# Nyström attention and a sticky mixture of experts: another order and another split of batch 0's steps

## The chip, the cores and the metric

One core of one Trainium2 chip runs the kernel. The metric is device time in microseconds of one execution; lower is better. Inputs lie in HBM in float32, and the output is written there in float32.

## The reference, cut

Attention with 32 landmarks per head, for 8 batches, 8 heads, 576 positions and 64 channels; A, Bm and C are softmaxes against landmark means, and Z is an iterated pseudo-inverse of Bm. A mixture of 8 experts follows, in which each token keeps its predecessor's expert unless its gate says otherwise.

```
q_lm, k_lm = means of q and k over 32 segments of 18
A  = softmax(scale * q    @ k_lm.T)      # 576 x 32 per head
Bm = softmax(scale * q_lm @ k_lm.T)      # 32 x 32
C  = softmax(scale * q_lm @ k.T)         # 32 x 576
Z  = Bm.T / (norm1(Bm) * norminf(Bm))
for _ in range(6): Z = 2 * Z - Z @ Bm @ Z
x = A @ Z @ C @ v                        # heads side by side: 576 x 512 per batch
logits, local = x @ w_gate, sigmoid(x @ w_local)
e[s] = argmax(logits[s]) if s == 0 or local[s] < 0.5 else e[s - 1]
out[s] = softmax(logits[s])[e[s]] * (relu(x[s] @ w1[e[s]]) @ w2[e[s]])
```

## The kernel before

All work is written out in one program under a manual order: each engine runs its instructions in the order in which the code issues them, and waits on semaphores for what it needs. For each batch the kernel finds the expert that most of its tokens have, runs that expert's two products for the whole batch (`expert`, with `mm1` for the hidden layer), and later runs the tokens of other experts in extra slots. It never forms x in full: W = Z C v and w1 are first multiplied into G (`w_w1`, and `first_w1` for the first 128 hidden units), so the hidden layer is A times G, in three products of high and low halves (`ath`, `atl`, `gh`, `gl`).

Batch 0's attention is written by hand in `startup`, and it has no other batch's work to hide behind. Its order is: loads of q, k and v of batch 0 and then of batch 1 on SP's queue; filler products on TensorE over zeros (L190, L192); landmark sums on VectorE (L261) and scores of C, Bm and A; then the Newton iteration (`newton` on TensorE, `newton_add` on VectorE, L1062) with the softmax of A between its steps (`sa_max`, `sa_exp`, `sa_sum`, `sa_norm`, `sa_back`). A lies in the tile `sa` in two groups of heads of 128 x 576; `sa_max` takes the maxima on VectorE (L1069) and subtracts them on GpSimd (L1070), `sa_exp` runs on ScalarE, `sa_sum` on VectorE (L1077), `sa_norm` inverts the sums on VectorE (L176, L177) and multiplies on GpSimd (L1081), `sa_back` transposes into `full` on VectorE (L1084). C times v (`c_v_rows`) goes to PSUM as `pv`, and u is `pv` over its sums, on ScalarE (L1127). From u come W, the gate's weights `wgc` (L760), the gate's logits (`gates`, L825), and `vote`, which writes the expert of the batch to `regs` (L875).

Around these steps stand pieces of batch 1's landmarks: `lk0`, `lq2` and `lk2` have halves on GpSimd (L310) and sums on VectorE (L313), `lq0` sums in pieces on VectorE (L294). `keep_busy` issues wide products over ones on TensorE (L930). The tile `firsts` (`w1f`, 2 MB) holds the first 128 hidden units of all eight experts, loaded before the expert is known.

Behind `regs`, SP reads the expert and issues the transfers of w1 (`load_w1`, L1232) and w2 (`load_w2`, L1274). `second_block`, at the simulated time 0.02, makes batch 1's scores of C (`c_products`, L621) and the second 128 units of G (`w_w1`, L1247, casts on ScalarE L1266, low halves `gl` on VectorE L1269); `c_max` takes maxima over those scores on VectorE (L631). `at_time` sets at which step of the expert's loop further pieces are issued; `fresh` (L847 `pe`, L849 `eq`) is one of them. GpSimd makes the low halves of w2 (`wl`, L1284).

## Time and profile before

| | us |
|---|---|
| median of 3 runs (451.6 to 452.22) | 451.7 |
| the profiled execution | 451.21 |
| its span, first to last instruction | 449.4 |
| TensorE busy in the span | 435.1 (97%) |
| VectorE | 284.5 (63%) |
| ScalarE | 216.0 (48%) |
| GpSimd | 192.0 (43%) |

The span is what the trace covers; the other 1.8 us lie around it. A matmul's end is modelled, so TensorE's busy share says little on its own; what counts is where it stands still and what it waits for.

### The profile page before, as it was taken

Reading aid. Unit: us, or ns where it says so; the run is one execution under the profiler, and the core shown is the slowest. Engines: PE = TensorE matmul, PEld = TensorE weight load, DVE = VectorE, ACT = ScalarE, POOL = GpSimd, SP = SyncE. Lnnn points to the kernel's source line nnn. Section 1 sums busy time; section 2 is a strip of 40 time slices with the busy share of each in tenths; the row PEclk is TensorE's granted clock in tenths of the full one; section 3 lists DMA queues with packets and bytes.
Section 4 is the critical chain, followed back from the end, with each engine's and each line's share of the span. In section 5 each row is a group of like instructions: output and inputs, shape, how many; then the busy total and the mean of one; then the engine's idle time right before and its main releaser. Section 6 shows DMA issues by size and latency. Waiting matters only on the chain.

```text
span 449.4 us, 12512 instructions
## 1 busy us (share of the span) xinstructions
PE 435.1 (97%) x4898; PEld 337.1 (75%) x4898; DVE 284.5 (63%) x869; ACT 216.0 (48%) x577; POOL 192.0 (43%) x235
## 2 busy tenths in 40 slices
PE   8888999999999999999999999999999999999996
PEld 3455777777786788878887788788887778776885
DVE  7878786666858576665766574656555786954111
ACT  2546525467354751566253752465145414445611
POOL 5456663165815664263632650174116601055520
PEclk9999999999999999999999999999999999999999
DMA  8959952779569697649957615831164315692211
GB/s 303 378 198 350 367 190 98 268 287 261 210 160 382 202 388 159 245 164 341 290 138 260 237 54 125 318 110 48 55 233 158 113 44 173 252 313 95 97 31 50
DMA packets 62365, 91.53 MB, mean 204 GB/s; under 512 B 26731, under 2 KB 28267, under 8 KB 61152
## 3 DMA queue, kind: packets, MB, share of 16 engines
q1 hardware_dynamic: 60960, 86.23, 57.0%
q0 software_dynamic: 1344, 4.48, 2.7%
q8 instruction: 39, 0.64, 0.6%
q14 instruction: 22, 0.18, 0.1%
HBM read 75.27 MB, written 15.47 MB: 202 GB/s over the span
## 4 chain that ended last, share of the span: by engine, by line
PE 77%; DVE 13%; ACT 5%; issue 2%; DMA 1%; POOL 1%; SPq 0%; DVEq 0%; ACTq 0%; POOLq 0%
PE py L1337 33%; PE ph L1295 19%; PE pg L1346 5%; PE ph L1247 2%; PE one L416 2%; PE one L463 1%; DVE h L1307 1%; PE one L562 1%; PE py L1573 1%; DMA k_t<-kT 1%; PE one L517 1%; DVE gl L1269 1%; PE one L825 1%; POOL t L265 1%; DVE sk L261 1%
## 5 line engine op out<-in xcount | busy, mean ns | idle before, releaser
L1337 PE MATMUL py<-wh,h 128*128 128x512 f32 x504 | 161.6, 403 | 0.1
L1284 POOL TENSOR_TENSOR wl<-raw,wh 128x512 fp32r<-128x512 f32 x64 | 82.2, 1293 | 70.8 <-ACT wh L1282 69.7
L1302 ACT ACTIVATE h<-ph 128x256 fp32r<-128x256 f32 (+1 forms) x128 | 52.4, 413 | 111.2 <-PE ph L1295 94.2
L1337 PEld LDWEIGHTS py<-wh,h 128*128 128x128 f32 x504 | 86.4, 189 | 25.2 <-issue 13.2
L1307 DVE SCALAR_TENSOR_TENSOR h<-ph,h 128x256 fp32r<-128x256 f32 x128 | 53.0, 416 | 61.0 <-ACT h L1302 58.2
L1337 PE MATMUL py<-wl,h 128*128 128x512 f32 x252 | 80.5, 400 | 0.0
L1295 PE MATMUL ph<-ath,gh 128*128 128x320 f32 (+1 forms) x256 | 77.5, 303 | 1.5 <-ACT gh L1266 0.8
L1295 PE MATMUL ph<-ath,gl 128*128 128x320 f32 (+1 forms) x256 | 75.8, 296 | 0.0
L1295 PE MATMUL ph<-atl,gh 128*128 128x320 f32 (+1 forms) x256 | 75.6, 295 | 0.0
L1295 PEld LDWEIGHTS ph<-ath,gh 128*128 128x128 f32 x256 | 48.4, 189 | 9.1 <-ACT h L1302 2.2
L1337 PEld LDWEIGHTS py<-wl,h 128*128 128x128 f32 x252 | 45.9, 188 | 11.6 <-issue 1.3
L1295 PEld LDWEIGHTS ph<-atl,gh 128*128 128x128 f32 x256 | 48.3, 189 | 3.9
L1295 PEld LDWEIGHTS ph<-ath,gl 128*128 128x128 f32 x256 | 48.3, 189 | 0.2 <-DVE gl L1269 0.2
L1282 ACT CAST wh<-raw 128x512 fp32r<-128x512 f32 x69 | 43.2, 627 | 2.2 <-DMA raw<-w 1.4
L1406 POOL TENSOR_TENSOR ys<-ys,yl 64x512 f32<-64x512 f32 x8 | 10.3, 1281 | 58.5 <-ACT yl L1404 58.5
L265 POOL TENSOR_TENSOR t<-q_t 128x288 f32<-128x288 f32 x20 | 14.5, 747 | 23.5 <-DVE sk L267 23.5
L423 DVE TENSOR_TENSOR et<-et,one 128x64 f32<-128x64 f32 x36 | 7.9, 220 | 24.7 <-ACT et L422 16.4
L794 POOL TENSOR_TENSOR sa<-sa,rsa 128x1152 f32<-128x1152 f32 x7 | 14.9, 2133 | 19.9 <-DVE s L693 13.2
L265 POOL TENSOR_TENSOR t<-k_t 128x288 f32<-128x288 f32 x22 | 17.0, 795 | 11.9 <-DVE sq L267 10.8
L1346 PE MATMUL pg<-wl,h 128*128 128x512 f32 x56 | 21.9, 391 | 0.0
L1346 PE MATMUL pg<-wh,h 128*128 128x512 f32 x56 | 21.8, 390 | 0.0
L1395 ACT ACTIVATE ys<-py,token 128x512 f32<-128x512 f32 x30 | 19.0, 685 | 5.0 <-PE py L1337 4.7
(435 smaller groups left out, 729.3 us busy)
## 6 DMA issues: line engine op xcount, KB each, us to landing
raw<-w SPq DMA_DIRECT2D x75, 256.0 KB
raw<-w SPq DMA_DIRECT2D x16, 1024.0 KB
k_t<-kT SPq DMA_DIRECT2D x9, 1152.0 KB
q_t<-qT SPq DMA_DIRECT2D x9, 1152.0 KB
out<-ys SPq DMA_DIRECT2D x31, 256.0 KB
v_t<-v SPq DMA_DIRECT2D x20, 256.0 KB
ad<-sa POOLq DMA_DIRECT2D x7, 576.0 KB, 3.1
v_t<-v SPq DMA_DIRECT2D x3, 1024.0 KB
```

The source lines that it names most:

```text
L265: nc.gpsimd.tensor_add(t9[:, i], src[:, a + i, :, 0:9], src[:, a + i, :, 9:18])
L416: return {1: lambda: each_place(lambda g, r: nc.tensor.matmul(pn[r, g, :], et[r, g, 0:32], et[r, g, n0:64], start=True, stop=True))}, part ...
L794: nc.gpsimd.tensor_tensor(out=sa, in0=sa, in1=rs.unsqueeze(2).broadcast_to([P, 2 * NJ, M]), op=ALU.mult)
L1282: by(out=wh, in_=raw)
L1284: rest.tensor_tensor(out=wl, in0=raw, in1=wh.bitcast(F32), op=ALU.subtract)
L1295: mm = nc.tensor.matmul(hp, w[:, g, c], x[:, g, s0:s0 + n], start=(i == 0), stop=(i == 5))
L1302: nc.scalar.activation(out=h[:, 0:e], in_=hp[:, 0:e], func=AF.Relu)
L1307: nc.vector.scalar_tensor_tensor(out=h[:, 384:384 + m], in0=hp[:, 0:m], scalar=0.0, in1=h[:, 0:m].bitcast(F32), op0=ALU.max, op1=ALU.subtract)
L1337: nc.tensor.matmul(yps[k], h[:, part + i * P:part + i * P + P], w, start=(f == 0 and part == 0 and w is wh), stop=(f == NC2 - 1 and part = ...
L1346: nc.tensor.matmul(yps[4], hs[ff][1], w, start=(ff == 0 and w is w2[ff][0]), stop=(ff == NC2 - 1 and w is w2[ff][1]))
L1395: nc.scalar.mul(out=ys, in_=yp, mul=st["pw"][:, k:k + 1])
L1406: nc.gpsimd.tensor_tensor(out=ys[0:64], in0=ys[0:64], in1=yl[0:64], op=ALU.add)
```

## The change

In words, in the order of the program. The fillers at the start become 12 wide and 35 narrow ones. The 2 MB preload into `firsts` is issued later in SP's queue, behind a one-element memset of that tile on GpSimd that stands after `lk0`'s two halves. Group 1 of A is subtracted, exponentiated, summed, scaled and transposed in two parts, of 9 and 9 of its 18 segments; the inverse of its sums stays one. The sums of C are reduced and inverted two Newton steps sooner. Newton's fourth addition and fifth step come ahead of A's first sum. u is made by one instruction on VectorE in place of two on ScalarE. `lq2`'s halves on GpSimd move behind A's products, and `lk0`'s sums on VectorE move between the transposes. Two fillers in place of three behind C times v; five wide fillers in place of three wide and 22 narrow ones behind the vote. w1's first half comes in two transfers in place of three, the second in one in place of two. `lq0`'s piece ahead of the gate moves behind the expert, where a single piece and a double one stand in place of two single ones. Batch 1's scores of C are issued in two halves, the second behind the second weight product, and the scores of the last 96 columns behind the product for blocks 2 and 3.

```diff
-    for _ in range(11):
+    for _ in range(12):
         nc.tensor.matmul(pz, zeros[:, 0:P], zeros, start=True, stop=True)
-    for _ in range(18):
+    for _ in range(35):
         nc.tensor.matmul(pz[:, 0:16], zeros[:, 0:P], zeros[:, 0:16], start=True, stop=True)
...
-    def c_products(st, k0, n):
+    def c_products(st, k0, n, places=range(4)):
...
-        for c in range(4):
+        for c in places:
...
         firsts = pre.tile([P, E, 512], F32, name="w1f")
-        nc.sync.dma_start(out=firsts, in_=w12[:, 0, :, 0:512].rearrange("e p x -> p e x"))
...
+        whole, first, second = slice(0, NJ), slice(0, 9), slice(9, NJ)
+
         def sa_max(g):
             nc.vector.reduce_max(out=mxa[:, g], in_=sa[:, g], axis=AX.X)
...
+        def sa_scaled(x, g, j, op):
+            nc.gpsimd.tensor_tensor(out=sa[:, g, j], in0=sa[:, g, j],
+                                    in1=x[:, g, j].unsqueeze(2).broadcast_to([P, j.stop - j.start, M]), op=op)
+
+        def sa_exp(g, j=whole):
+            nc.scalar.activation(out=sa[:, g, j], in_=sa[:, g, j], func=AF.Exp, scale=scale)
+
+        def sa_sum(g, j=whole):
+            nc.vector.reduce_sum(out=rsa[:, g, j], in_=sa[:, g, j], axis=AX.X)
+
+        def sa_back(g, j=whole):
+            nc.vector.transpose(out=full[:, g, M * j.start:M * j.stop], in_=sa[:, g, j].rearrange("p j l -> p (j l)"))
...
         sa_max(0)
+        sa_scaled(mxa, 0, whole, ALU.subtract)
         lk0_half(0)
         lk0_half(1)
+        nc.gpsimd.memset(firsts[0:1, 0, 0:1], 0.0)
+        nc.sync.dma_start(out=firsts, in_=w12[:, 0, :, 0:512].rearrange("e p x -> p e x"))
...
         c_turn(4, 1)
+        nc.vector.reduce_sum(out=sums[:, 2:4], in_=sc, axis=AX.X)
+        nc.vector.reciprocal(out=sums[:, 2:4], in_=sums[:, 2:4])
...
         sa_max(1)
+        sa_scaled(mxa, 1, first, ALU.subtract)
+        sa_scaled(mxa, 1, second, ALU.subtract)
+        sa_exp(0)
         c_v_rows(st, pv, 0, range(3, 5))
         c_v_rows(st, pv, 1, range(0, 2))
-        sa_exp(0)
-        sa_sum(0)
         newton_add(4)
         newton(5)
-        nc.vector.reduce_sum(out=sums[:, 2:4], in_=sc, axis=AX.X)
-        nc.vector.reciprocal(out=sums[:, 2:4], in_=sums[:, 2:4])
+        sa_sum(0)
+        sa_exp(1, first)
         c_v_rows(st, pv, 1, range(2, 5))
         idle = ph.tile([P, 512], F32, name="ph")
-        keep_busy(3, idle)
+        keep_busy(2, idle)
+        newton_add(5)
+        inverse(rsa[:, 0], 1e-9)
+        sa_scaled(rsa, 0, whole, ALU.mult)
+        u = st["u"] = sm.tile([P, 2, D], F32, name="u")
+        nc.vector.tensor_tensor(out=u, in0=pv, in1=sums[:, 2:4].unsqueeze(2).broadcast_to([P, 2, D]), op=ALU.mult)
+        sa_exp(1, second)
+        sa_sum(1, first)
+        sa_sum(1, second)
+        inverse(rsa[:, 1], 1e-9)
+        sa_scaled(rsa, 1, first, ALU.mult)
+        sa_scaled(rsa, 1, second, ALU.mult)
         lq2_half(0)
-        sa_norm(0)
-        newton_add(5)
-        sa_exp(1)
-        u = st["u"] = sm.tile([P, 2, D], F32, name="u")
-        for g in range(2):
-            nc.scalar.mul(out=u[:, g], in_=pv[:, g], mul=sums[:, 2 + g:3 + g])
-        sa_sum(1)
-        sa_norm(1)
         lq2_half(1)
         sa_back(0)
-        lk0(0)
...
-        lq0(1)
+        sa_back(1, first)
+        lk0(0)
         newton_gate(0, st)
         keep_busy(2, idle)
-        sa_back(1)
+        sa_back(1, second)
+        lk0(1)
         a_high(1)
...
-        lk0(1)
...
         vote(st, lq0)
-        keep_busy(3)
-        pz = one.tile([P, 512])
-        for _ in range(22):
-            nc.tensor.matmul(pz[:, 0:16], ones, ones[:, 0:16], start=True, stop=True)
+        keep_busy(5)
...
-        st["w1", 0] = load_w1(e, 0, ((nc.sync, 1, 1, 0, P), (nc.sync, 2, 1, 0, P), (nc.sync, 3, 1, 0, P)))
+        st["w1", 0] = load_w1(e, 0, ((nc.sync, 1, 1, 0, P), (nc.sync, 2, 2, 0, P)))
...
-        st["w1", 1] = load_w1(e, 1, ((nc.sync, 0, 2, 0, P), (nc.sync, 2, 2, 0, P)))
+        st["w1", 1] = load_w1(e, 1)
...
         lq0(1)
-        lq0(1)
+        lq0(2)
...
-            c_products(nx, 0, 512)
+            c_products(nx, 0, 512, (0, 1))
             lk2(0)
             lk2(1)
             g1 = w_w1(st, 0, 1, 1, ((py, "py"), (py, "py")))
             next(g1)
-            c_products(nx, 512, 96)
+            c_products(nx, 0, 512, (2, 3))
             c_max(nx, 1, (0,))
             at_once(g1)
...
         at_time(1.005, lambda: at_once(w_w1(st, 0, 2, 2, ((py, "py"), (py, "py")))))
+        at_time(1.007, c_products, nx, 512, 96)
```

VectorE, before, from the maximum over A's group 1 to the transpose of group 0 (`yl` holds Newton's matrices, `mxa` and `rsa` the maxima and sums of A):

```order
L1069 TENSOR_REDUCE mxa<-sa 128x18
L1077 TENSOR_REDUCE rsa<-sa 128x18
L1062 TENSOR_TENSOR yl<-ph,yl 128x2x64
L1116 TENSOR_REDUCE sums<-sc_239 128x2
L1117 RECIPROCAL sums<-sums 128x2
L176 TENSOR_SCALAR rsa<-rsa 128x18
L177 RECIPROCAL rsa<-rsa 128x18
L1062 TENSOR_TENSOR yl<-ph,yl 128x2x32
L1077 TENSOR_REDUCE rsa<-sa 128x18
L176 TENSOR_SCALAR rsa<-rsa 128x18
L177 RECIPROCAL rsa<-rsa 128x18
L1084 STREAM_TRANSPOSE at<-sa 128x576
```

The same stretch of VectorE in the changed kernel:

```order
L1070 TENSOR_REDUCE mxa<-sa 128x18
L1061 TENSOR_TENSOR yl<-ph,yl 128x2x64
L1080 TENSOR_REDUCE rsa<-sa 128x18
L1061 TENSOR_TENSOR yl<-ph,yl 128x2x32
L176 TENSOR_SCALAR rsa<-rsa 128x18
L177 RECIPROCAL rsa<-rsa 128x18
L1130 TENSOR_TENSOR u<-pg,sums 128x128
L1080 TENSOR_REDUCE rsa<-sa 128x9 x2
L176 TENSOR_SCALAR rsa<-rsa 128x18
L177 RECIPROCAL rsa<-rsa 128x18
L1083 STREAM_TRANSPOSE at<-sa 128x576
L1083 STREAM_TRANSPOSE at<-sa 128x288
```

Newton's addition now stands between the maximum and the sum, the sums of C have left, u has come in behind the first inverse, and group 1's sum and transpose are in parts.

GpSimd, before, from the first subtraction of A to the low half of A (`h` are batch 1's landmark halves):

```order
L1070 TENSOR_TENSOR sa<-sa,mxa 128x576
L310 TENSOR_TENSOR h<-k_t_229 128x288 x2
L1070 TENSOR_TENSOR sa<-sa,mxa 128x576
L310 TENSOR_TENSOR h<-q_t_228 128x288
L1081 TENSOR_TENSOR sa<-sa,rsa 128x576 x2
L310 TENSOR_TENSOR h<-q_t_228 128x288
L1148 TENSOR_TENSOR atl<-at,ath 128x576
```

The same stretch of GpSimd in the changed kernel:

```order
L1073 TENSOR_TENSOR sa<-sa,mxa 128x576
L310 TENSOR_TENSOR h<-k_t_247 128x288 x2
L1096 MEMSET w1f 1x1
L1073 TENSOR_TENSOR sa<-sa,mxa 128x288 x2
L1073 TENSOR_TENSOR sa<-sa,rsa 128x576
L1073 TENSOR_TENSOR sa<-sa,rsa 128x288 x2
L310 TENSOR_TENSOR h<-q_t_246 128x288 x2
L1155 TENSOR_TENSOR atl<-at,ath 128x576
```

The memset has come in behind the first landmark halves, the other two halves have moved behind all of A's products, and group 1 is in parts.

TensorE, before, behind the first hidden product of batch 0 (`one` and `pg` receive batch 1's scores, `py` the product with w1):

```order
L1295 MATMUL ph<-atl,gh 128x320
L1295 MATMUL ph<-ath,gl 128x320
L621 MATMUL one<-k_t_229,ql 32x512 x8
L1247 MATMUL py<-raw_620,wt 32x128 x8
L621 MATMUL one<-k_t_229,ql 32x96
L621 MATMUL pg<-k_t_229,ql 32x96
```

The same stretch of TensorE in the changed kernel:

```order
L1301 MATMUL ph<-ath,gl 128x320
L621 MATMUL one<-k_t_247,ql 32x512 x4
L1253 MATMUL py<-raw_620,wt 32x128 x8
L621 MATMUL one<-k_t_247,ql 32x512 x4
L1301 MATMUL ph<-ath,gh 128x320
L1301 MATMUL ph<-atl,gh 128x320
L1301 MATMUL ph<-ath,gl 128x320
```

Half of the wide scores now stand behind the weight product, and the narrow ones have left this place. Each float32 product of this list runs as two in the trace.

## Rows read from the trace of the kernel before

**Rows 1.** Windows: length, busy us of PE PEld DVE ACT POOL, clock, DMA, GB/s

```profile
18.00:24.00 6.00, 5.24 (x154) 2.92 (x154) 5.35 (x16) 2.83 (x8) 5.51 (x7) 1.00 0.97 353
...
36.00:42.00 6.00, 4.97 (x36) 3.17 (x36) 4.80 (x20) 4.55 (x21) 3.97 (x5) 1.00 1.02 371
42.00:48.00 6.00, 6.00 (x76) 3.94 (x78) 5.20 (x19) 3.53 (x11) 3.98 (x5) 1.00 1.03 406
```

**Rows 2.** Chain of waits: start us, length us, engine, tile, line

```profile
7.33 0.37 DVE nm L977
```

**Rows 3.** Timeline of TensorE at the start: start us, length us, instruction, count

```profile
1.23 4.88 PE L190 MATMUL one<-sa 128*128 128x512 bf16 x11 [1.23 <-DVE sa L180]
...
5.90 0.65 PE L192 MATMUL one<-sa 128*128 128x16 bf16 x18
...
6.49 0.69 PE L965 MATMUL one<-k_t,ql 64*32 64x288 f32 x8
```

**Rows 4.** Timeline, 19 to 26 us, all engines

```profile
19.06 0.74 DVE L1069 TENSOR_REDUCE mxa<-sa 128x18 f32<-128x576 f32 x1
...
19.71 0.74 DVE L1077 TENSOR_REDUCE rsa<-sa 128x18 f32<-128x576 f32 x1
19.88 1.16 POOL L1070 TENSOR_TENSOR sa<-sa,mxa 128x576 f32<-128x576 f32 x1
20.37 0.28 DVE L1062 TENSOR_TENSOR yl<-ph,yl 128x128 f32<-128x128 f32 x1
...
20.84 0.23 DVE L176 TENSOR_SCALAR rsa<-rsa 128x18 f32<-128x18 f32 x1
...
20.99 0.74 POOL L310 TENSOR_TENSOR h<-q_t 128x288 f32<-128x288 f32 x1
...
21.66 0.50 ACT L1127 ACTIVATE u<-pg,sums 128x64 f32<-128x64 f32 x2
21.70 1.16 POOL L1081 TENSOR_TENSOR sa<-sa,rsa 128x576 f32<-128x576 f32 x1
...
22.20 0.42 PE L1134 MATMUL ph<-u,yl 32*32 32x64 f32 x16
...
22.57 0.31 DVE L176 TENSOR_SCALAR rsa<-rsa 128x18 f32<-128x18 f32 x1
...
24.74 0.77 DVE L1084 STREAM_TRANSPOSE at<-sa 128x576 f32<-128x576 f32 x1
...
25.96 0.52 PE L825 MATMUL pg<-at,wgc 128*32 128x128 f32 x10 [0.46 <-issue]
```

**Rows 5.** Single lines' instructions: ns min/median/max, first and last start us

```profile
L176 DVE TENSOR_SCALAR rsa<-rsa x9: 182/184/311, 20.8 to 354.2; 128x36 f32<-128x36 f32 x7, 128x18 f32<-128x18 f32 x2
...
L849 DVE SCALAR_TENSOR_TENSOR eq<-pe,keys x8: 199/201/1344, 37.6 to 367.3; 128x40 f32<-128x40 f32 x8
...
L621 PE MATMUL one<-k_t,ql x24: 242/589/613, 31.5 to 32.8; 64*32 64x512 f32 x16, 64*32 64x96 f32 x8
```

**Rows 6.** Timeline, from the expert to 40 us, all engines

```profile
28.19 0.80 DVE L294 TENSOR_REDUCE sq<-q_t 128x16 f32<-128x288 f32 x2
...
29.00 1.43 SPq L1232 DMA_DIRECT2D raw<-w  x3
...
32.39 0.45 PE L1247 MATMUL py<-raw,wt 64*32 64x128 f32 x16
...
32.64 0.69 DVE L631 TENSOR_REDUCE nm8c<-one 128x1 f32<-128x512 f32 x1 [0.86 <-PE one L621]
...
33.25 0.48 DVE L1269 TENSOR_TENSOR gl<-py,gh 128x128 fp32r<-128x128 f32 x2
...
37.58 1.29 POOL L1284 TENSOR_TENSOR wl<-raw,wh 128x512 fp32r<-128x512 f32 x1
37.59 1.34 DVE L849 SCALAR_TENSOR_TENSOR eq<-pe,keys 128x40 f32<-128x40 f32 x1
...
39.94 0.59 PE L1247 MATMUL ph<-raw,wt 64*32 64x512 f32 x1 [0.97 <-DVE atl L1310]
```

More of the change, by code (lines that the diff above doesn't have):

```diff
@@ L1066, in startup @@
         full = st["full"] = at.tile([P, 2, S], F32, name="at")
+        whole, first, second = slice(0, NJ), slice(0, 9), slice(9, NJ)
         def sa_max(g):
             nc.vector.reduce_max(out=mxa[:, g], in_=sa[:, g], axis=AX.X)
-            nc.gpsimd.tensor_tensor(out=sa[:, g], in0=sa[:, g], in1=mxa[:, g].unsqueeze(2).broadcast_to([P, NJ, M]),
-                                    op=ALU.subtract)
-        def sa_exp(g):
-            nc.scalar.activation(out=sa[:, g], in_=sa[:, g], func=AF.Exp, scale=scale)
-        def sa_sum(g):
-            nc.vector.reduce_sum(out=rsa[:, g], in_=sa[:, g], axis=AX.X)
-        def sa_norm(g):
-            inverse(rsa[:, g], 1e-9)
-            nc.gpsimd.tensor_tensor(out=sa[:, g], in0=sa[:, g], in1=rsa[:, g].unsqueeze(2).broadcast_to([P, NJ, M]), op=ALU.mult)
-        def sa_back(g):
-            nc.vector.transpose(out=full[:, g], in_=sa[:, g].rearrange("p j l -> p (j l)"))
+        def sa_scaled(x, g, j, op):
[7 more added lines that the diff above has]
+            nc.vector.transpose(out=full[:, g, M * j.start:M * j.stop], in_=sa[:, g, j].rearrange("p j l -> p (j l)"))
         lq0 = landmark_parts(nx, "q", 0)
```

## The prediction

> **What bounds the kernel now.** I read the windows table first, then the chain of waits and the timeline of the first 45 us, then the instructions of three lines on their own. From 42 us on a window of 6 us holds 6.00 us of TensorE work; the one before holds 4.97, the startup's like it [rows 1]. Past 42 us TensorE waits for nothing that this diff touches, so what the diff does before that point moves the end by as much, with its sign. The profiled execution took 451.21 us for a span of 449.4; the median of the runs is 451.7, half a microsecond above it. I make the sum as shifts against the profiled execution and put the same shifts on the median, because that is what will be compared.
>
> The startup is one serial chain over VectorE, TensorE, ScalarE and GpSimd up to the batch's expert (`regs`), then a second one from the expert to about 40 us. I take the parts in that order.
>
> **Filler at the start.** The fillers stand ahead of the first scores on TensorE: 11 wide ones from 1.23 to 5.90, 0.42 us each, then 18 narrow ones in 0.59, and at 6.49 the first scores follow directly [rows 3]. The maximum over those scores stands on VectorE ahead of the sums of the second half of q and k, and the chain of waits runs through it at 7.33 [rows 2]. So VectorE takes over each delay of these scores. The change adds one wide filler and 17 narrow ones. The narrow ones cost 17 x 0.59/18 = 0.56 at most; the wide one 0.42 at 1.2 GHz (512 columns in 0.42 us, as the eleven before it) or half of that at 2.4 GHz. Ends 0.65 and 1.0; I take 0.8, the middle. A cost of nothing would need data that arrive later than in this execution. Cost **+0.8**.
>
> **Newton, A's sums and u, up to the expert.** Before, A's sum stands ahead of Newton's fourth addition: maximum at 19.06, sum at 19.71 (each 0.74), addition at 20.37 [rows 4]. Now the addition follows the maximum, at 19.72, which is 0.65 sooner; the last product starts 0.05 behind its end, at 20.06, with the sum beside it (19.92 to 20.66), and the last addition comes at 20.6. Then the inverse (0.2 and 0.3) and u on VectorE, 128x128 from PSUM like the addition at 20.37, so 0.28: u ends at 21.45 where ScalarE's two ended at 22.16 (21.66 + 0.50), and the product with u, at 22.20 before, can start at 21.5: 0.7 sooner. That is not yet the gain, because the gate products also need all of A, whose transpose was the later of the two (24.74 + 0.77 = 25.51) [rows 4]. For A I count GpSimd again. A half of 288 elements I price at 0.74, as the 128x288 row at 20.99, against 1.16 for 576: the split adds 0.32 per step. The tiny memset for the preload takes 0.1. So: halves of the subtraction 19.97 to 21.45, group 0's product to 22.65, group 1's inverse ready at 23.0, its halves to 23.8 and 24.55. VectorE transposes group 0 (0.77) from 22.9, then the first half (0.4), one landmark sum (0.4, half of the 0.80 for two at 28.19 [rows 6]), the gate's copy (0.2), and the second half (0.4): A is complete at 25.05. Gain **-0.45** on the expert.
>
> Bounds. After A's end TensorE stood 0.45 us longer (25.51 to 25.96, a row with "issue" [rows 4]); if that stall goes too, the gain is 0.9. The other end is the inverse. Its first instruction, a median of 0.18, took 0.31 at 22.57 and ended at 22.88, just when GpSimd's operation of 21.70 + 1.16 = 22.86 did [rows 4, 5]. With two halves back to back it can be kept off until 21.4; then u gives 0.2 instead of 0.7 and A ends at 25.35: a gain of 0.15.
>
> **After the expert.** The landmark sums behind it on VectorE grow from two pieces (0.80) to one of the same size and a double one, 0.4 + 0.74, so ScalarE's scale and its first cast of G come 0.35 later. That is hidden: only 8 of 16 score products now stand ahead of the second weight product on TensorE (at 32.39, [rows 6]), which frees 0.45, and that product waits for its transfer anyway. Five wide fillers in place of three and 22 narrow ones end some 0.2 sooner; the same casts hide that.
>
> But the other 8 score products now come behind the weight product. VectorE's maximum over them stood at 32.64, with `gl` behind it at 33.25 [rows 6]; in the new order both keep their places, and the maximum cannot start until products that begin at 32.64 and take 0.59 [rows 5] have ended: 33.3, and `gl` at 33.9, 0.65 later. The hidden layer's third product waits for `gl`, the weight product for blocks 2 and 3 stands behind it, and the next `gl` behind that. The 8 small products (512 to 575) that moved away lie in a later TensorE wait and give nothing. The 0.65 then meets the wait at 39.94, where TensorE stands for 0.97 until VectorE is through [rows 6]. There `eq` took 1.34 us from 37.59, next to GpSimd's `wl` from 37.58 to 38.87; its median over the batches is 0.20 [rows 5, 6]. If VectorE comes 0.65 later it finds the same `wl`, stands at `pe` instead of `eq` until 38.87, and is through some 0.35 later than before, not 0.65. Ends: nothing, and the full 0.65. Cost **+0.35**.
>
> The Trainium skill has a rule for this pair, on its page "SBUF — State Buffer", section "Who interferes with whom": VectorE and GpSimd share one pair of SBUF ports, a VectorE instruction with two SBUF inputs, or one in a two-port mode, contends with GpSimd, and whoever comes second is shut out for the other's whole instruction. The rows at 22.57 and 37.59 agree with it: both ended as GpSimd's did. Without it 1.34 us would be read as the price of `eq`, and the cost here would be 0.65 instead of 0.35.
>
> **Transfers.** Held back behind GpSimd's memset (after the two landmark halves, so at 20 + 0.8) the preload's 2.1 MB begin at about 22 and at the 353 GB/s of that stretch [rows 1] take 5.9 us: there at 28. TensorE needs it about when SP issues the first weights, at 29.00 before [rows 6] and 29.35 now. The stores of A and W, 0.7 MB, follow to 29.9, as the first weights' bytes begin. Cost nothing, at most 0.5 where these overlap. Fewer, larger transfers of w1 save issue time on SP, but the engines are full there (share 1.02 from 36 to 42 us [rows 1]), and the product for blocks 2 and 3 needed both anyway: nothing.
>
> **Sum.** 0.8 - 0.45 + 0.35 = +0.7: 451.9 in a profiled execution, **452.4** against the median of 451.7. That is +0.15%, and about 0.2%, 0.9 us, is what a measurement of this kernel can tell from no change.
>
> **Rivals.**
> (a) Slower: GpSimd's halves keep VectorE's inverse off until 21.4, as worked out above. It decides if the second half starts before the inverse asks, about 20.7; both are due within 0.1 us. Then u and A give 0.1 instead of 0.45: 0.8 - 0.1 + 0.35 = +1.05, 452.75; with `gl`'s 0.65 in full 453.05. The row at 22.57 speaks for it; against it, the same instruction at 20.84 (0.23) got in between GpSimd's operation to 21.04 and the next at 20.99 [rows 4].
> (b) The filler costs nothing, because the first scores wait for data beyond 7.2 us in the runs that count, so that part of the change does nothing: 0 - 0.45 + 0.35 = -0.1, 451.6. The half microsecond between the profiled execution and the median leaves room for it; the rows of this execution are against it.
> (c) VectorE reaches `pe` and `eq` while GpSimd is not in `wl`. Then the 1.14 us over the usual 0.20 go: 0.8 - 0.45 + 0.65 - 1.14 = -0.15, 451.55. It needs `wl` to move against VectorE by half a microsecond or more, so the second w2 tile's transfer to land that much sooner or later against the expert.
> (d) Faster: the filler is free, the 0.45 at 25.51 goes too (a gain of 0.9), and the cost after the expert is nothing: -0.9, 450.8; with (c)'s saving 450.3. Taken as 450.6. It needs three things at once.
>
> **Chances.** Forecast 0.40, (a) 0.25, (b) 0.17, (c) 0.10, (d) 0.08. The forecast stands near the upper bound of 0.2%, so 0.12 of its 0.40 counts as slower; of (a) 0.22 is slower; of (b) 0.04 and of (c) 0.03 are faster, and all of (d). Faster 0.15, the same 0.51, slower 0.34. The range 450.9 to 453.4 leaves out (d) with 0.08, and 0.12 above, where the filler takes its 1.0 and `gl` its 0.65 together with (a), or the transfers collide.
>
> **What would show it.** In the new profile the first scores start at about 7.3 instead of 6.49 and the sums of k end 0.8 later: right on the filler. u ends 0.5 to 0.7 sooner against the maximum over A, and A's last transpose 0.45 sooner: right on the middle part; an inverse of 0.7 us or more speaks for (a). Between the expert and the weight product at 39.94 there are 0.35 us more, with the maximum behind the second half of the score products; an `eq` of 0.2 there and no long `pe` speaks for (c). I am wrong if the first scores start below 6.8, or if TensorE's granted clock falls during the startup.

## The result, and the profile after

The changed kernel takes **455.31 us** (454.56 to 455.73, 4 runs) against 451.96 for the kernel before measured with it: ratio 1.0075, 95% interval 1.0056 to 1.0095. So it is slower by 0.75%; I had forecast 452.4, about the same. Measured again on another chip it is 455.75 against 451.88, ratio 1.0093 (1.0075 to 1.0110). The profiled execution took 455.62 for a span of 453.8, 4.4 more than the span of before.

First the stretches of 6 us, answering to [rows 1]: busy time of each engine, TensorE's granted clock, the DMA engines' share and rate.

```profile
18.00:24.00 6.00, 5.27 (x170) 3.03 (x170) 5.74 (x15) 2.84 (x7) 4.66 (x8) 1.00 0.49 133
24.00:30.00 6.00, 3.72 (x43) 1.59 (x37) 5.35 (x16) 2.62 (x8) 5.13 (x7) 1.00 1.00 320
42.00:48.00 6.00, 5.44 (x67) 3.48 (x67) 4.41 (x15) 4.28 (x15) 2.17 (x3) 1.00 1.01 377
```

One stretch of the kernel before, which [rows 1] leave out:

```profile
24.00:30.00 6.00, 5.06 (x80) 3.22 (x80) 4.59 (x15) 2.99 (x10) 4.22 (x6) 1.00 0.34 128
```

The DMA engines stand half idle from 18 to 24 (0.49, 133 GB/s, where before it was 353), and are full from 24 to 30, when they were a third busy before (0.34). That is the preload, moved. The stretch that was full of TensorE work from 42 us on starts later by what was lost.

The timeline of the changed kernel, from the start to the second hidden product:

```profile
1.23 4.32 PE L190 MATMUL one<-sa 128*128 128x512 bf16 x12 [1.23 <-DVE sa L180]
5.39 1.02 PE L192 MATMUL one<-sa 128*128 128x16 bf16 x35
6.35 0.69 PE L964 MATMUL one<-k_t,ql 64*32 64x288 f32 x8
...
19.67 0.28 DVE L1061 TENSOR_TENSOR yl<-ph,yl 128x128 f32<-128x128 f32 x1
20.66 0.51 DVE L176 TENSOR_SCALAR rsa<-rsa 128x18 f32<-128x18 f32 x1
21.38 0.23 DVE L1130 TENSOR_TENSOR u<-pg,sums 128x128 f32<-128x128 f32 x1
22.00 1.16 POOL L1073 TENSOR_TENSOR sa<-sa,rsa 128x576 f32<-128x576 f32 x1 [0.87 <-DVE rsa L1080]
22.36 0.83 DVE L176 TENSOR_SCALAR rsa<-rsa 128x18 f32<-128x18 f32 x1
25.16 0.47 DVE L1083 STREAM_TRANSPOSE at<-sa 128x288 f32<-128x288 f32 x1
26.26 0.35 DVE L833 STREAM_TRANSPOSE lg<-pg 128x160 f32<-128x160 f32 x1 [0.30 <-PE pg L832]
26.28 1.41 POOL L1155 TENSOR_TENSOR atl<-at,ath 128x576 fp32r<-128x576 f32 x1
26.87 0.87 DVE L866 TENSOR_TENSOR ohb<-lg,mxl 128x40 bf16<-128x40 f32 x1
28.34 0.15 DVE L875 TENSOR_SCALAR regs<-best 128x1 int32<-128x1 int32 x1
30.85 0.91 PE L1263 MATMUL py<-w1f,ys 128*128 x6 [1.66 <-POOL h L310]
33.88 0.19 PEld L1253 LDWEIGHTS py<-raw,wt 64*32 64x32 f32 x16 [0.72 <-DMA raw<-w]
33.89 0.45 PE L1253 MATMUL py<-raw,wt 64*32 64x128 f32 x16
34.16 1.04 PE L621 MATMUL one<-k_t,ql 64*32 64x512 f32 x8
35.25 0.69 DVE L631 TENSOR_REDUCE nm8c<-one 128x1 f32<-128x512 f32 x1 [1.92 <-PE one L621]
35.86 0.28 DVE L1275 TENSOR_TENSOR gl<-py,gh 128x128 fp32r<-128x128 f32 x1
...
161.99 0.29 PE L517 MATMUL one<-k_t,ql 64*32 64x160 f32 x1 [1.16 <-issue]
```

And four rows of the kernel before that [rows 3 to 6] don't have:

```profile
28.12 0.15 DVE L875 TENSOR_SCALAR regs<-best 128x1 int32<-128x1 int32 x1
29.31 1.13 PE L1257 MATMUL py<-w1f,ys 128*128 x8 [0.24 <-ACT ql L275]
31.46 1.09 PE L621 MATMUL one<-k_t,ql 64*32 64x512 f32 x16
32.39 0.18 PEld L1247 LDWEIGHTS py<-raw,wt 64*32 64x32 f32 x16 [0.75 <-DMA raw<-w]
```

Against these and [rows 3 to 6] the shift goes like this: nothing at the first scores (6.35 for 6.49), 0.70 sooner at the addition that the prediction calls Newton's fourth (19.67 for 20.37), 0.2 later at the expert (28.34 for 28.12), **1.54 later at the first weight product** (30.85 for 29.31), 1.50 later at the second weight product (33.89 for 32.39), and **2.61 later at the maximum over the scores** (35.25 for 32.64). From there the shift stays 2.6 until 158 us, where a wait of 1.16 stands in the middle of one loop's products and makes it 4.0; 0.2 more comes near 218 us. The second profile of the same kernel has the same steps: 3.3, then 4.6 behind a wait of 1.17 at 162.61, then 4.8.

The row at 30.85 names GpSimd as releaser, but that work is no operand of the product. In the second profile the row names the right one:

```profile
31.60 0.57 PE L1263 MATMUL py<-w1f,ys 128*128 x3 [1.82 <-DMA w1f<-w]
```

By the semaphore events the preload's last bytes landed at 30.72 in the first profile and 31.46 in the second, 0.13 and 0.14 ahead of the product (25.67 before).

The second weight product waits for a transfer too, its own w1 block `raw`, in both kernels (0.72 and 0.75). That block was issued only 0.22 later, at 29.22 for 29.00, but landed 1.5 later, at 33.84 for 32.35: 4.6 us after its issue instead of 3.35, behind the bytes of the preload and the two stores. So the late preload is met twice, and the second product would have come late even if the first had not waited.

### The profile page after: what moved, and what is told of

Read it like the earlier page. It is cut to its first block, busy times and chain, and to the rows that moved or that the text cites. A ratio compares the mean times of both kernels' runs of the same rounds, so it can differ in the third digit from the quotient of the medians.

```text
span 453.8 us, 12505 instructions
## 1 busy us (share of the span) xinstructions
PE 435.3 (96%) x4895; PEld 336.8 (74%) x4895; DVE 286.0 (63%) x871; ACT 216.0 (48%) x576; POOL 192.2 (42%) x238
## 4 chain that ended last, share of the span: by engine, by line
PE 76%; DVE 13%; ACT 5%; issue 2%; POOL 2%; DMA 1%; SPq 0%; DVEq 0%; ACTq 0%; POOLq 0%
PE py L1343 33%; PE ph L1301 19%; PE pg L1352 5%; PE ph L1253 2%; PE one L416 2%; PE one L463 1%; PE one L562 1%; DVE h L1313 1%; PE py L1579 1%; DMA k_t<-kT 1%; PE one L517 1%; PE one L825 1%; POOL t L265 1%; DVE gl L1275 1%; PE ph L1558 1%
```

## The experiments

Theory **P**: the late preload costs what the first weight product waits. **S**: the split of the score products delays the maximum and `gl`. **C**: TensorE waits for its own instructions at some places, and the change moves these. Rivals stand in each expectation. Ratios are to the kernel before on the same chip, with 95% intervals.

| run | from | edit | ratio | interval |
|---|---|---|---|---|
| e1 | changed | preload early | 1.0024 | 1.0015 to 1.0033 |
| e2 | changed | scores whole | 1.0084 | 1.0066 to 1.0101 |
| e3 | changed | both | 1.0025 | 1.0011 to 1.0038 |
| e4 | before | preload late | 1.0049 | 1.0031 to 1.0068 |
| e5 | changed | nothing | 1.0093 | 1.0075 to 1.0110 |
| e6 | before | Newton, A, u | 1.0008 | 0.9996 to 1.0020 |
| e7 | before | filler | 1.0024 | 1.0013 to 1.0035 |
| e8 | before | 34 instructions fewer | 1.0021 | 0.9999 to 1.0043 |
| e9 | before | score halves | 1.0020 | 1.0011 to 1.0029 |
| e10 | before | preload in halves | 0.9995 | 0.9986 to 1.0004 |
| e11 | e6 | preload in halves | 1.0019 | 1.0008 to 1.0030 |
| e12 | before | w1 transfers | 1.0000 | 0.9991 to 1.0008 |
| e13 | before | preload at 16.5 us | 1.0016 | 1.0003 to 1.0030 |
| e14 | before | half a preload, late | one run, 450.99 us | |
| e15 | e11 | q's halves behind `atl` | 1.0004 | 0.9993 to 1.0016 |

### The preload: e1 to e5

In e1 the edit on the changed kernel is this; e2 puts the score products back, e3 does both.

```diff
         firsts = pre.tile([P, E, 512], F32, name="w1f")
+        nc.sync.dma_start(out=firsts, in_=w12[:, 0, :, 0:512].rearrange("e p x -> p e x"))
...
-        nc.gpsimd.memset(firsts[0:1, 0, 0:1], 0.0)
-        nc.sync.dma_start(out=firsts, in_=w12[:, 0, :, 0:512].rearrange("e p x -> p e x"))
```

> The changed kernel with the preload of the experts' first weight block issued at its old place, ahead of the loads of batch 1, without the memset that held it back. Theory P: in the changed kernel the first weight product (30.85 us) waited for that preload, which landed at 30.72; with it early the product starts at about 29.3 to 29.5 and the time falls by 1.5, from 455.3 to 453.8. Rival W: GpSimd's work behind the expert holds the product, as the row's releaser says (landmark differences on GpSimd); then it stays at 30.5 or later and the time at 455.0 or more. Rival C: the rest of the loss is a wait of TensorE for its own instructions (1.16 us at 160.8 in the profiled execution); if that wait goes with any shift of the schedule, the fall is up to 2.7, to 452.6.

> The changed kernel with the 16 large score products of the next batch in one block ahead of the second weight product, and the small ones in their old place. Theory S: VectorE's maximum over the scores no longer waits behind the weight product, the second gl comes 1.05 sooner against the weight product (as before: 0.86 behind it instead of 1.97), and the time falls by 1.0 to 454.3. Rival: the loss at 33 to 36 us is the late landing of the weights passed on, so nothing falls: 455.2.

> The changed kernel with the preload early and the score products whole. Theory P+S: the two losses add, 1.5 + 1.05, 452.75; without the wait of TensorE for instructions at 160 us another 0.6 to 1.2 less, 451.6 to 452.1. If both act on one wait, they don't add: 453.5 or more.

The reverse on the kernel before, e4, and the changed kernel once more, e5:

```diff
         firsts = pre.tile([P, E, 512], F32, name="w1f")
-        nc.sync.dma_start(out=firsts, in_=w12[:, 0, :, 0:512].rearrange("e p x -> p e x"))
...
         lk0_half(0)
         lk0_half(1)
+        nc.gpsimd.memset(firsts[0:1, 0, 0:1], 0.0)
+        nc.sync.dma_start(out=firsts, in_=w12[:, 0, :, 0:512].rearrange("e p x -> p e x"))
```

> The kernel before with nothing changed but the preload, held back behind the memset as in the changed kernel. Theory P: the preload lands at about 30.7, the first weight product moves from 29.31 to about 30.8, the time from 452.0 to 453.5. As I had predicted for this part: there at 28, nothing, 452.0 to 452.5. If the low rate of the preload came from the changed GpSimd and VectorE work beside it, it lands at 29.5 or sooner here.

> The changed kernel once more, unchanged, so that it is measured beside the parts below. Theory P: 0.75% over the kernel before as at first (3.3 us), the preload landing at 30 to 31 us and the first weight product behind it. If the loss comes mostly from the half-clock stretch that TensorE falls into in some runs while it waits, the profiles differ from run to run by 1.5 us and this one shows such a stretch near 30 us. If the wait of TensorE for its instructions at 161 us belongs to the program, it stands there again; if it is chance, it is gone or elsewhere.

**That the late preload costs holds from both sides.** Taken back, it gives 0.5 to 0.7% (1.0024 against 1.0075 and 1.0093, on other chips); done alone it costs 0.49%, 2.2 us, the largest part. In e4 the expert is even 0.60 sooner than before (27.52), and the first weight product still 0.4 later. The price is not that wait alone, as P has it: in the four profiles with the whole preload late (the changed kernel's two, e2, e4) w1's first block landed 4.2 to 4.6 us after its issue, and 3.2 to 3.5 us after it in all the others. The first two rows are e4's timeline, then comes a window (granted clock third from the right).

```profile
27.52 0.15 DVE L875 TENSOR_SCALAR regs<-best 128x1 int32<-128x1 int32 x1
29.71 1.88 PE L1258 MATMUL py<-w1f,ys 128*128 x8 [1.23 <-DMA w1f<-w]
...
30.00:36.00 6.00, 5.81 (x68) 4.48 (x67) 2.93 (x10) 1.61 (x7) 0.69 (x1) 0.73 0.90 272
```

After the wait of 1.23 TensorE's granted clock fell from 2.4 to 1.2 GHz from 29.88 to 33.30 (mean 0.73 in the window): the eight products took 1.88 instead of 1.13. So a wait can be followed by a second price in some executions; in both profiles of the changed kernel the clock stayed at 1.00, and there was none. In e1 it fell from 25.06 to 28.47, behind a wait of 0.84 inside the product of W with the gate's weights (L757).

e2 and e3 give no support to S: with the scores whole the changed kernel was no faster in the median (1.0084), though in e2's profile the maximum comes 1.1 sooner (34.14); with the preload early the pair e1 and e3 is equal. e2 doesn't refute S either: its interval holds a gain of 0.2% against the changed kernel's 1.0093, and its profile is of the fastest of its six executions (451.57; median 453.70). e9 below says otherwise.

### The parts alone: e6, e7, e9, e12

e6 is the kernel before with the change's order of Newton's steps, A's halves, `u` on VectorE, and the landmark sums and fillers that go with them, everything else as before. e7, e9 and e12 are these edits on the kernel before:

```diff
-    for _ in range(11):
+    for _ in range(12):
...
-    for _ in range(18):
+    for _ in range(35):
```

```diff
-            c_products(nx, 0, 512)
+            c_products(nx, 0, 512, (0, 1))
...
-            c_products(nx, 512, 96)
+            c_products(nx, 0, 512, (2, 3))
...
+        at_time(1.007, c_products, nx, 512, 96)
```

```diff
-        st["w1", 0] = load_w1(e, 0, ((nc.sync, 1, 1, 0, P), (nc.sync, 2, 1, 0, P), (nc.sync, 3, 1, 0, P)))
+        st["w1", 0] = load_w1(e, 0, ((nc.sync, 1, 1, 0, P), (nc.sync, 2, 2, 0, P)))
...
-        st["w1", 1] = load_w1(e, 1, ((nc.sync, 0, 2, 0, P), (nc.sync, 2, 2, 0, P)))
+        st["w1", 1] = load_w1(e, 1)
```

> The kernel before with one part of the change: Newton's fifth step ahead of A's sum, A's second group in two halves, u on VectorE, and the order of landmark sums and fillers that goes with it; preload, fillers at the start, weight transfers and scores as before. As I predicted it: A complete 0.45 sooner, 0.45 less, 451.5 against 452.0 or the same fraction. Rival A: the halves on GpSimd shut VectorE's second inverse out (0.83 us in the changed kernel), A's last transpose ends no sooner than 25.5, and a wait of TensorE for its own instructions (0.8 us at the W product in the two kernels with this part and an early preload) adds to it: slower by 0.5 to 1.0.

> The kernel before with one part of the change: 12 wide and 35 narrow zero products at the start in place of 11 and 18. As I predicted: the first scores at 7.3 instead of 6.49, 0.8 slower. Rival: the price hangs on when the full clock is granted, which differs from run to run (4.4 us in the changed kernel's profile, 6.1 in the one of before, 7.0 in a later one); with an early grant the fillers end before the data are there and cost nothing, so the mean over runs is 0 to 0.5.

> The kernel before with one part of the change: 8 of the 16 large score products ahead of the second weight product and 8 behind it, the small ones in a later wait. Theory S, from the changed kernel's profile (maximum and gl 1.05 later against the weight product): the maximum over the scores moves from 32.64 to about 33.6, gl likewise, and the time rises by 0.65 to 1.05, 0.15 to 0.23%. Rival: as the pair of kernels with an early preload gave it (451.41 against 451.36), nothing within 0.3 us, since the wait at 39.94 takes it up.

> The kernel before with one part of the change: the first weights in two transfers of 1 and 2 blocks instead of three of 1, and the second half's in one instead of two. As I predicted: nothing, within 0.2%. Rival: the products that wait for a block (32.39 us, 15 of 16 engines through by 31.42) get it later when it is part of a larger transfer, up to 0.7 later, 0.15% slower.

The filler costs 0.24%, 1.1 us; the score halves 0.20%, 0.9; Newton's part nothing that can be told (0.08%); the transfers of w1 nothing. With e4's 0.49 the parts add up to 1.01%, against 0.75 and 0.93 measured for the whole, enough to make up the whole. But the parts don't simply add: without the preload they make 0.52%, and e1, which has them all together, costs 0.24 (0.15 to 0.33). e7's first scores and a wait later in it, and e9's maximum behind the second half of the products with a wait later in it:

```profile
1.24 4.88 PE L190 MATMUL one<-sa 128*128 128x512 bf16 x12 [1.24 <-DVE sa L180]
5.95 1.02 PE L192 MATMUL one<-sa 128*128 128x16 bf16 x35
6.90 0.69 PE L965 MATMUL one<-k_t,ql 64*32 64x288 f32 x8
...
PE ph L1247 <- DMA raw<-w: 1.8, 1, 1.8
```

```profile
32.13 0.45 PE L1248 MATMUL py<-raw,wt 64*32 64x128 f32 x16
32.40 1.04 PE L621 MATMUL one<-k_t,ql 64*32 64x512 f32 x8
33.50 0.69 DVE L631 TENSOR_REDUCE nm8c<-one 128x1 f32<-128x512 f32 x1 [2.03 <-PE one L621]
...
38.95 0.20 DVE L849 SCALAR_TENSOR_TENSOR eq<-pe,keys 128x40 f32<-128x40 f32 x1
40.15 0.59 PE L1248 MATMUL ph<-raw,wt 64*32 64x512 f32 x1 [0.33 <-issue]
...
PE one L449 <- issue: 1.2, 1, 1.2
```

In e7's profile the first scores start 0.41 later and the expert comes 0.25 later. The other 0.85 of the 1.1 that it is late at the weight product of 39.94 (41.04) stands in the wait of 1.8 for a w1 transfer, whose last bytes landed at 40.90 (39.53 before). Whether the filler makes that landing late no run shows.

In e9 the maximum starts 1.37 behind the weight product, before 0.25 [rows 6]. Here `eq` met no `wl` and took 0.20, my rival (c), so the weight product at 40.15 is only 0.2 later than before's 39.94. The median says 0.9 (0.5 to 1.3). In e9's profile the shift stays at 0.2 to 0.3 up to 207 us, and the rest comes there, from the wait of 1.2 at 209.20 for TensorE's own instructions (next section). A stall at the same instruction stands in e7, e10, e12 and e13 too (0.5 to 0.9), and not in the one profile of the kernel before; e12, whose profile has it, costs nothing in the median. So how much of the 0.9 is the score halves' own, and why e2 and e3 don't show the part at all, stays open.

### TensorE's instructions: e8 and e10

The wait of 1.16 at 161.99 stands between two products of one loop that wait for nothing. The trace holds the packets that bring instructions, 16 KB each: one landed at 160.56, 1.4 ahead of the end of that wait. In the kernel before one landed at 24.60, and the "issue" stall inside the gate products [rows 4] ended at 25.96, 1.36 later. e8 takes 34 instructions out ahead of it (18 narrow fillers less and one wide one more, each a product and a weight load):

```diff
-    for _ in range(11):
+    for _ in range(12):
...
-    for _ in range(18):
-        nc.tensor.matmul(pz[:, 0:16], zeros[:, 0:P], zeros[:, 0:16], start=True, stop=True)
```

> The kernel before with 12 wide zero products at the start and no narrow ones, 34 instructions fewer on TensorE (a matmul and a weight load each). Theory C: TensorE stands where a 16 KB block of its instructions has to come in by DMA (25.51 to 25.96 in the kernel before, inside the gate products, the block having landed at 24.60); with 34 instructions fewer the place moves behind the gate products, into the fillers, and the stall leaves the path: VectorE's copy of the logits comes 0.4 sooner, 0.3 to 0.5 less in all. Rival: the stall is at the gate products whatever the count (it waits for A's transpose or a bank); then it stays there, and the time is within 0.2 of before.

> The kernel before with the preload in two transfers: experts 0 to 3 at the old place, experts 4 to 7 held back as in the changed kernel. Theory P and C together: the second half starts on queues that are still busy, so it runs at the old rate and is there by 27, the first weight product doesn't wait (29.3); and TensorE's next block of instructions, which stood behind the whole preload (landing at 24.60), comes in sooner, so the 0.45 us stall inside the gate products goes: 0.3 to 0.5 less than before. Rival: the block still comes in at 24 or later, or the second half at the low rate lands behind 29.3: same as before, or 1 us slower.

e10's edit is the two halves:

```diff
-        nc.sync.dma_start(out=firsts, in_=w12[:, 0, :, 0:512].rearrange("e p x -> p e x"))
+        nc.sync.dma_start(out=firsts[:, 0:4], in_=w12[0:4, 0, :, 0:512].rearrange("e p x -> p e x"))
...
+        nc.gpsimd.memset(firsts[0:1, 4, 0:1], 0.0)
+        nc.sync.dma_start(out=firsts[:, 4:8], in_=w12[4:8, 0, :, 0:512].rearrange("e p x -> p e x"))
```

The waits of TensorE in e8, and the gate products in e13 (below) and in e10:

```profile
PE pg L671 <- issue: 2.0, 1, 2.0
PE ph L515 <- issue: 1.3, 1, 1.3
```

```profile
26.55 0.52 PE L825 MATMUL pg<-at,wgc 128*32 128x128 f32 x10 [1.05 <-issue]
```

```profile
25.10 0.98 PE L825 MATMUL pg<-at,wgc 128*32 128x160 f32 x16
27.63 0.15 DVE L875 TENSOR_SCALAR regs<-best 128x1 int32<-128x1 int32 x1
```

Counted in the trace's records of TensorE, the stalls stand at the 450th, 706th, 3522nd (e4), 4290th and 5570th instruction, all multiples of 256 apart, in whatever product that is: at the 706th in every kernel whose preload is whole and issued by 16.5 us (in the gate products or at L757) except e8, and in none whose preload is late or halved. There the block of instructions lands by 20.5 to 22.3, instead of at 23.3 to 25.1 behind the preload. In the kernel before the 450th instruction ran at 19.3 and the packet with the next block began only at 23.21; in the changed kernel, whose queues were nearly empty, the times are 18.9 and 19.61. (The waits called "issue" at the weight product of 39.94, 0.3 to 1.2 us in five profiles, stand at that product and not at a count; they are not among these.) The Trainium skill says, on its page "Runtime: NRT & Kernel Launch", section "Instruction fetch mechanics", that instructions come in 16 KiB blocks of 256 and that crossing into the next is mostly hidden. The size agrees (39 packets of 16 KB for some 9,900 records); here the crossings named cost 0.2 to 2.0 us.

So C is right on the place and wrong on the worth. e8's stall at the gates went, and two others came, at the 450th (2.0) and the 4290th (1.3), with a fall of the clock (0.84 from 18 to 24); its runs lie between 450.5 and 456.05. With fewer instructions ahead the fetch moves as well: the 194th instruction, 256 ahead of the 450th, ran at 15.4 instead of 13.3, and the block for the 450th landed at 20.42 instead of 16.57. e10 has the expert 0.5 sooner (27.63), keeps that to 207 us and loses it to a stall at the 5570th instruction: the same as before.

### Why the late preload is slow: e13, e14

e13 takes the issue from its old place, as e4 does, and puts it here:

```diff
         newton_add(0)
+        nc.vector.memset(firsts[0:1, 0, 0:1], 0.0)
+        nc.sync.dma_start(out=firsts, in_=w12[:, 0, :, 0:512].rearrange("e p x -> p e x"))
```

> The kernel before with the preload held back a shorter time, behind a memset on VectorE that follows Newton's first addition, so issued at about 16.5 us, with some 3.5 us of the loads of batch 1 still on the queues. If the late preload is slow because it starts on idle queues: full rate, landing at 25.7 to 26.2, the first weight product at 29.3, the same time as before. If it is slow because it was issued late whatever stands before it: landing at 28 or later and packets of 100 ns and more.

e14 is e4 with `firsts[:, 0:4]` and `w12[0:4, ...]` in the late transfer; it leaves out the blocks of experts 4 to 7.

> The kernel before with the late preload of experts 0 to 3 alone (the other four blocks are left out, so what is computed is not the reference's where an expert above 3 is chosen). If each late transfer pays a start of some 3 us at a low rate and then runs at 350 GB/s: 1 us to start, 3 at 200, then 0.45 MB more, landing at about 25.5. If the rate is low throughout (2.1 MB in 9.8 us): first packets at 20.9 and 4.9 us, landing at 25.8, with packets of 105 ns and more to the end. The two differ in the packets' durations at the end, 88 against 105 ns, not in the landing.

First the changed kernel's windows of 1 us (share and rate of the DMA engines at the end), then e14's, then one of the kernel before.

```profile
20.00:21.00 1.00, 1.00 (x53) 0.71 (x42) 1.00 (x3) 0.44 (x1) 1.00 (x2) 1.00 0.05 14
21.00:22.00 1.00, 0.76 (x18) 0.27 (x16) 0.97 (x5) 0.44 (x1) 0.13 (x1) 1.00 0.72 129
22.00:23.00 1.00, 0.79 (x11) 0.28 (x4) 0.97 (x2) 0.62 (x2) 1.00 (x1) 1.00 0.92 264
24.00:25.00 1.00, 0.58 (x8) 0.09 (x2) 0.79 (x3) 0.83 (x3) 1.00 (x3) 1.00 0.91 211
27.00:28.00 1.00, 0.33 (x8) 0.20 (x7) 1.00 (x2) 0.00 (x0) 0.69 (x1) 1.00 1.06 369
```

```profile
22.00:23.00 1.00, 1.00 (x20) 0.38 (x18) 0.97 (x2) 0.47 (x3) 1.00 (x1) 1.00 0.93 229
25.00:26.00 1.00, 0.95 (x21) 0.53 (x20) 0.87 (x2) 0.94 (x4) 1.00 (x2) 1.00 0.94 357
```

```profile
21.00:22.00 1.00, 1.00 (x32) 0.56 (x27) 0.62 (x4) 0.93 (x3) 1.00 (x3) 1.00 1.04 385
```

The queues are nearly empty from 18 to 21 (14 to 33 GB/s). From 21 on the engines are busy, but the preload's 2 KB packets take 183, 114 and 105 ns on average where they take 88 in the kernel before; the rate reaches 369 GB/s only at 27. From 22 on half of the packets take 84 ns or less, so a minority that takes several times as long makes the mean. The rate falls again at 24 to 26 (143 and 129 ns), behind the issues of W's store at 23.71 and A's at 24.96. In e14 the packets come down to 84 ns three microseconds after the first, and half the bytes land at 26.21, 6.2 us from issue; all of them take 10.85. e13 contradicts the reading that it is the idle queues: issued at 16.52 onto queues still full, the packets that ran from 18 to 22 took 103 to 121 ns on average and the transfer landed at 27.14. (Its 0.16% is no wait for the preload: the first weight product follows the expert as closely as before, and the expert is 0.58 late behind the stall of 1.05.) Before, the preload was issued at 10.25, 7.4 us before its first bytes ran. So the slow packets are those of a preload that runs within some microseconds of its issue. A late issue alone does not make packets slow, though: w1's first packets, issued at 29.00 in the kernel before, took 90 and 96 ns from 30 to 32. What slows the packets no row names.

### Where Newton's gain went: e11, e15

> The kernel before with Newton's, A's and u's part of the change, and the preload in two transfers as in the last one. With A complete at 25.37 (that part alone) and without the instruction stall behind it (25.60 to 25.95 there), the logits come 0.5 sooner than before and the time falls by 0.4 to 0.6, 0.1%. Rival: the gain of this part is lost behind the expert whatever the stall does (landmark sums of a double piece stand ahead of the scale): same as before.

e15 moves two calls in it:

```diff
-        lq2_half(0)
-        lq2_half(1)
...
         a_low(0)
+        lq2_half(0)
+        lq2_half(1)
```

> The kernel before with Newton's, A's and u's part and the preload in two transfers (as one before it, 0.19% slower than the kernel before), and with the two landmark halves of q on GpSimd moved behind A's low part. GpSimd is then in the low part from about 24.95 to 26.35 and in the halves, 0.74 each, after it; VectorE's one-hot comparison at 26.87 is shut out for 0.25 at most instead of 0.65. If that lock ate the gain: the comparison takes 0.25 to 0.45, the expert comes 0.4 to 0.6 sooner than in that kernel (28.34), and the time falls by 0.1%, to 0.1% over the kernel before or less. If not: the expert stays at 28.3.

VectorE in e11 and in e15:

```profile
26.88 0.87 DVE L866 TENSOR_TENSOR ohb<-lg,mxl 128x40 bf16<-128x40 f32 x1
28.35 0.15 DVE L875 TENSOR_SCALAR regs<-best 128x1 int32<-128x1 int32 x1
```

```profile
27.13 0.22 DVE L866 TENSOR_TENSOR ohb<-lg,mxl 128x40 bf16<-128x40 f32 x1
27.95 0.15 DVE L875 TENSOR_SCALAR regs<-best 128x1 int32<-128x1 int32 x1
```

In e11, e2 and both profiles of the changed kernel `ohb` takes 0.87 to 0.89, because GpSimd is in `atl` from 26.3 to 27.7 (26.9 to 28.3 in e5); with `atl` moved ahead it takes its usual 0.22. e15's expert comes 0.4 sooner than e11's although its startup ran 0.25 later, and the ratio falls from 1.0019 to 1.0004. The two intervals overlap, and in the profiles another 0.7 us of the gain comes at `eq`, which met no `wl` in e15 (0.20) and did in e11 (1.33), so the ratio is not the price of `ohb` alone. No version beats the kernel before.

## Why the prediction was wrong, step by step

**Filler, +0.8: right in size, in part by luck.** Alone it costs 1.1 us (0.6 to 1.6), but in e7's profile only 0.25 of it goes the way that I forecast, through the first scores to the expert; the rest stands in the wait for w1. I had said I would be wrong if the first scores started below 6.8, and in the changed kernel's profile they start at 6.35. The reason is none that I gave: the full clock was granted at 4.43 us there and at 6.13 in the profile of before, so the wide products from there on started 0.21 apart instead of 0.42. In the profiles of the other kernels with these fillers the grant came between 3.9 and 7.0, and the first scores between 6.3 and 7.4: the sum let the grant decide over one wide product, and it decides over as many as stand behind it.

**Newton, A and u, -0.45: wrong.** The first half is right: addition 0.70 sooner, `u` through at 21.61 instead of 22.16. A's last transpose was to end at 25.05 and ended at 25.63. My rival (a) had the mechanism, and in part the place: the first inverse took 0.51 until 21.17, as GpSimd's two halves ended at 21.13. But the larger loss was at the second, shut out for 0.83 by GpSimd's whole product of group 0 (22.00 to 23.16). The logits came 0.43 sooner all the same, since the stall of [rows 4] went: I had it as a bound, and it was a block of instructions. Then `ohb` lost 0.65 to `atl`, an operation that I had not looked at, because the change doesn't touch it; it moves it. Here too VectorE ended (27.74) as GpSimd did (27.69). Alone (e6) this part is 0.08% slower, not clear of no change, where I had it 0.1% faster.

**After the expert, +0.35: too small.** I let 8 score products take 0.59, the duration of one [rows 5]; the eight together took 1.04, nearly what all sixteen took before (1.09), so the split freed nothing ahead of the weight product either, where I had counted 0.45. The maximum came 1.1 later against that product, not 0.65. The lock at `eq` moved to `wide`, as my step had it in kind: in the changed kernel `eq` took 0.49 and `wide` 1.06, so nothing was given back. Alone the part costs 0.9 (0.5 to 1.3), of which e9's profile shows 0.2 to 0.3 ahead of 207 us; that undoing it in the changed kernel gave nothing in the median is not explained.

**Transfers, nothing: the step that failed.** I took 353 GB/s from a stretch in which the transfer had been waiting on the queue for 7 us and more, and had it there at 28. It began at 20.9, sooner than the 22 that I had, but took 9.8 us instead of 5.9: it landed at 30.7 and 31.5, and its price is 0.49% alone, 2.2 us, where I had allowed 0.5. The overlap with the first weights that I let cost 0.5 at most put w1's first block 1.5 later. With that term at 2.2, Newton's at 0.35, the halves at 0.9 and the filler at 1.1, the sum is 4.6 us, 1.0%. That w1's transfers cost nothing was right.

**Past 42 us: wrong too.** I had TensorE wait there for nothing that the diff touches. In both profiles of the changed kernel the stall for instructions at 162 us adds 1.3 to the shift, and the kernel before has none there.

Rival (b), the filler free, happened in the one profile; (a) happened in kind, mostly at another instruction, and (c) in e9 but not in the changed kernel; (d) did not. (In (a) I put the gain at 0.1, where my bound for the same case gave 0.15; it decides nothing.) None of them had the late preload, so the range was too low altogether.

## What to carry to other kernels

Price a transfer that is moved from rows in which it was issued as late as it will be, not from the rate of one that waited long on full queues, and keep it well ahead of its need; half of it early was enough here. Look too at which transfers then queue behind it. When a step comes sooner, look at which operation of another engine then overlaps the last small instructions of the chain, whether or not the change touches it. A term smaller than a microsecond can be paid back hundreds of microseconds later by a stall for instructions, so read the gain at the end of the span and not only where it arises.

## What the runs showed of the hardware

- TensorE's instructions come in blocks of 256 by DMA, 16 KB each. Where TensorE stalled for a block, for 0.2 to 2.0 us, the block's packet had landed 1.2 to 1.7 us before the stall ended, and the stall stood at the 450th, 706th, 3522nd, 4290th or 5570th instruction, whatever the kernel had there.
- The granted clock rose to 2.4 GHz between 3.9 and 7.0 us in executions with nearly the same start, and in three profiles (e1, e4, e8) it fell to 1.2 GHz for 3.4 us, each time behind a wait of TensorE of 0.84 to 2.0 us. In the changed kernel, waits of 1.7 and 1.8 us brought no fall.
- The 2 KB packets of the preload took 88 ns on average when it had been issued 7.4 us before they ran, and 103 to 187 ns (means over 1 us) in the first 3 to 4 us of one that ran within 1.5 us of its issue.
